# First MLP of a fused attention and two-MLP kernel: softmax steps, squares and conversions in other slots, and all four sums of a half batch cleared by ACT

## The chip, the cores and the metric

The kernel runs on one core of a Trainium2 chip. The metric is device time in microseconds of one execution; lower is better. The engines are TensorE (PE, with its weight loads as PEld), VectorE (DVE), ScalarE (ACT) and SyncE (SP), which issues the DMAs. Each takes its instructions in the order in which the program has them.

## The reference

Attention in two steps (32 packed queries per head gather k and v, then q attends to the result), an MLP with squared ReLU, and an MLP with x times sigmoid(1.702 x). Everything is float32; w_in, w_out and their second pair come in as 64-bit numbers.

```
s = scale * q k^T;  a = exp(s - max);  a = a / (sum(a) + 1e-9)       # sm_attn
p_packed = sm_attn(p, k, v)            # 8 batches, 8 heads, 32 x 64
out = sm_attn(q, p_packed, p_packed)   # 8 batches, 8 heads, 576 x 64
x = out as (4608, 512)
h = max(x @ w_in, 0);  x = (h * h) @ w_out          # w_in 512 x 2048, w_out 2048 x 512
h = x @ w_in2;  out = (h * sigmoid(1.702 h)) @ w_out2
```

## The kernel before

A matrix product in float32 is made from three products of split numbers (`prod`, L79): hi by hi, hi by lo and lo by hi. The split of a number is an ACT copy (hi) and a DVE subtraction (lo), as in `split` (L74).

**First MLP, up to 788 us.** The product of p_packed with w_in is folded first: for each batch `m_step` (L364) makes M, four pieces f of 512 columns, from p_packed and w_in, so that h is M times the attention weights a. Tokens go by half batches of 288, the 2048 hidden columns by 16 blocks `fc` of 128. A *slot* is one (half batch, block). The main loop at the end of the function issues, slot by slot: the split of the block two slots ahead (`gsplit`, L391), the first product, ReLU and square of the block three slots ahead (`mm1`, L378: six matmuls into a bank, relu L386, square L388, both on ACT), the second product of this slot's block (`mm2`, L395: twelve matmuls, three into each of four banks `y`), and then what the plan holds for the slot. After the last block of a half batch `mm2` empties the four banks into `ysb` and stores it. The next block's first matmul into a bank waits for that.

From batch 2 on a batch is 32 slots: slots 0 to 15 for the first half, 16 to 31 for the second. Beside them runs the attention of the next batch, in the slots that a list `steps` (L742) gives, counted from the batch's first slot: `s1`, `s1b` (first scores and their exponentials), `tr`, `pv`, `t2` (p_packed and its transposes), then for each half `s2a` (scores of q, transposed and less their maximum, on DVE), `s2b` (exponential on ACT, L344, then sum, reciprocal, multiplication and transpose on DVE, L346 to L355) and `s2c` (split into a), and `m_step` for the four f. In batches 0 and 1 (table `first`, L684) the halves are cut into eight blocks and w_in and w_out are still being converted from 64 bits; there `ysb` is a sum with what was stored before (L414, DVE).

The w_in pieces for `m_step` are read back by `load_win` into three buffers, two pieces per f: n = 0 to 2 ahead, the others in the slots of the `m_step`s that free a buffer.

Also beside the batches run the conversions of the second MLP's weights (`convert`): two ACT and four DVE instructions each (L118 to L129), and the sums and splits of weight parts (`unit_sums`, `unit_hi` on ACT, L190, `unit_lo` on DVE, L195, each followed by a store to w_d from one of three buffers). They stand in slots that are not 14, 15 or 0 of 16.

**Second MLP, from 788 us.** Tokens go by five pairs of blocks (512 or 384 each side) with a seven-product scheme: `y_sum` makes four differences of the input on DVE (T1 to T4, L481), `y_hi` and `y_lo` split them (L489 on ACT, L492 on DVE), `mm_a` and `mm_b` are the products, `keep_a` (L554) empties a bank on ACT, and `g_sum`, `g_hi`, `g_lo` (L511, L516, L492) make the operands of the second product. `at2(t0 + dt, ...)` puts a step dt product-steps from the pair's first.

Of the kernel before, what the change touches and what calls it, by code (L numbers as in the profile page):

```python
# [13 lines left out]
AF = mybir.ActivationFunctionType  # L14
ALU = mybir.AluOpType
# [8 lines left out]
HS = S // 2  # L24
NFC = DFF // P
# [18 lines left out]
def fused_kernel(ctx, tc, qT, kT, vv, pT, w_in, w_out, w_in2, w_out2, out):  # L44
# [7 lines left out]
    nc = tc.nc  # L52
# [337 lines left out]

    def gsplit(b, hf, fc, seg):  # L391
# [3 lines left out]
    def mm2(b, hf, fc, seg):  # L395
# [281 lines left out]
    wps = []  # L677


    for f, *a in (*loads(0)[:6], (ahead,), loads(0)[6], (ahead,), (load_q, 0, 0, 0), (load_q, 0, 1, 0), (ahead,),  # L680
                  (load_q, 0, 2, 0), (load_q, 0, 3, 0), (ahead,), *((load_q, 0, hp, 1) for hp in range(4))):
        at(S0, f, *a)

    first = {  # L684
# [15 lines left out]
        5: [(tr, 1, 0), (convert,)],  # L700
# [14 lines left out]
        22: [(convert,)],  # L715
        23: [(convert,)],
        25: [(convert,)],
        26: [(convert,)],
        27: [(convert,), (convert,)],
        30: [(m_step, 0, 3), (convert,)],  # L720
        33: [(convert,)],
        35: [(convert,)],
        43: [(m_step, 1, 2)],
        46: [(m_step, 1, 3)],
    }
    for s, steps in first.items():
        for f, *a in steps:
# [67 lines left out]
    for p in range(NP2):  # L797
# [93 lines left out]
```

## Time and profile before

| | us |
|---|---|
| median of 3 runs | 1491.49 (1489.2 to 1492.52) |
| the profiled execution, by its own time | 1491.68 |
| its span, first to last instruction | 1489.5 |
| busy: PE, DVE, ACT | 1435.9, 973.9, 846.6 |
| mean granted TensorE clock, share of full | 0.984 |

The span is what the trace covers; some 2 us of the device time lie around it. Busy times of different engines lie beside each other and are not to be added. PE's busy time counts matmuls whose ends are modelled, so waits show better than busy shares do. All times below are from the start of the span.

### The profile page before, as it was taken

The page shows a single profiled execution, that of the slowest core. Times are in us where ns is not written, and L with a number is a line of the kernel's source. Part 1 is how long each engine was busy: PE and PEld are TensorE (multiplying, and loading weights), DVE is VectorE, ACT ScalarE, POOL GpSimd, SP SyncE. Part 2 cuts the span into 40 slices and gives each one's busy share as a digit, 9 for nine tenths or more (in the row PEclk, how much of TensorE's full clock was granted, in tenths as well). Part 3 has the DMA queues.
Part 4 walks back from the last instruction along what each step waited for, and adds up shares of the span by engine and source line. Part 5 has one row for each costly group of instructions (what it writes and reads, how often), then busy time and mean ns, then how long its engine had stood idle before and what let it go on. Part 6 is the DMA issues. An engine that isn't in the chain of part 4 may idle for free.

```text
span 1489.5 us, 25122 instructions
## 1 busy us (share of the span) xinstructions
PE 1435.9 (96%) x9786; PEld 1281.5 (86%) x9786; DVE 973.9 (65%) x1684; ACT 846.6 (57%) x1760; POOL 0.7 (0%) x6
## 2 busy tenths in 40 slices
PE   7899999999999998999999999999999999999998
PEld 4678989888898897889998888788878888999998
DVE  6898465756756666573235687668775776677585
ACT  4888667567676766665565463446344634454452
POOL 0000000000000000000000000000000000000000
PEclk8999999999999999999999999999999999999999
DMA  9756657476465664633044566556765576677775
GB/s 310 248 171 219 206 180 235 149 234 199 163 215 185 213 205 161 204 134 123 17 151 164 197 218 250 207 188 221 263 215 197 211 244 237 248 286 284 256 285 174
DMA packets 110774, 307.95 MB, mean 207 GB/s; under 512 B 9024, under 2 KB 52032, under 8 KB 96576
## 3 DMA queue, kind: packets, MB, share of 16 engines
q1 hardware_dynamic: 110656, 306.35, 60.3%
q8 instruction: 77, 1.26, 0.3%
q14 instruction: 41, 0.34, 0.1%
HBM read 250.94 MB, written 55.38 MB: 206 GB/s over the span
## 4 chain that ended last, share of the span: by engine, by line
PE 74%; DVE 14%; ACT 5%; DMA 4%; issue 2%; SPq 0%; ACTq 0%; DVEq 0%
PE h L85 33%; PE y L85 22%; PE o L85 14%; DVE hid L511 2%; PE m L256 2%; ACT g L516 2%; DMA w_d<-wc 1%; DVE g L492 1%; PE s L256 1%; DVE yT L481 1%; DVE y L492 1%; DMA wA<-w_d 1%; DVE o L593 1%; DVE gh L77 1%; PE pv L314 1%
## 5 line engine op out<-in xcount | busy, mean ns | idle before, releaser
L85 PE MATMUL y<-gh,wo 128*128 128x288 f32 x3072 | 461.2, 300 | 24.3 <-ACT ysb L418 14.7
L85 PEld LDWEIGHTS y<-gh,wo 128*128 128x128 f32 x3072 | 431.1, 192 | 28.6 <-ACT ysb L418 17.1
L85 PE MATMUL h<-y,wA 128*128 128x512 f32 (+1 forms) x1680 | 350.2, 368 | 4.7 <-ACT r L554 3.4
L85 PE MATMUL o<-g,wB 128*128 128x512 f32 (+1 forms) x1680 | 348.9, 367 | 0.3 <-DMA wB<-w_d 0.3
L85 PEld LDWEIGHTS h<-y,wA 128*128 128x128 f32 x1680 | 305.4, 188 | 46.6 <-ACT r L554 5.5
L85 PEld LDWEIGHTS o<-g,wB 128*128 128x128 f32 x1680 | 305.7, 188 | 39.8 <-DMA wB<-w_d 0.6
L85 PE MATMUL h<-a,M 128*128 128x288 f32 x1536 | 263.2, 307 | 10.7 <-ACT a L360 3.8
L85 PEld LDWEIGHTS h<-a,M 128*128 128x128 f32 x1536 | 221.8, 193 | 56.4 <-issue 27.6
L516 ACT ACTIVATE g<-hid 128x1024 fp32r<-128x1024 f32 (+1 forms) x140 | 132.8, 971 | 146.8 <-DVE hid L511 120.3
L77 DVE TENSOR_TENSOR gh<-gf,gh 128x288 fp32r<-128x288 f32 x256 | 114.9, 452 | 112.6 <-ACT gh L76 112.3
L492 DVE TENSOR_TENSOR g<-hid,g 128x1024 fp32r<-128x1024 f32 (+1 forms) x140 | 152.7, 1115 | 54.5 <-ACT g L516 53.6
L386 ACT ACTIVATE r<-h 128x288 f32<-128x288 f32 x256 | 103.8, 406 | 102.8 <-PE h L85 102.3
L554 ACT ACTIVATE r<-h 128x512 f32<-128x512 f32 (+1 forms) x120 | 66.5, 554 | 116.6 <-PE h L85 114.5
L562 DVE TENSOR_TENSOR hid<-h,r 128x512 f32<-128x512 f32 (+1 forms) x120 | 76.0, 634 | 74.4 <-PE h L85 62.6
L388 ACT ACTIVATE gf<-r 128x288 f32<-128x288 f32 x256 | 113.9, 445 | 8.1
L76 ACT ACTIVATE gh<-gf 128x288 fp32r<-128x288 f32 x256 | 111.8, 437 | 1.8
L572 DVE TENSOR_TENSOR hid<-hid,sg 128x512 f32<-128x512 f32 (+1 forms) x120 | 75.9, 632 | 47.2 <-ACT sg L568 47.2
L373 DVE TENSOR_TENSOR M<-m,M 128x512 fp32r<-128x512 f32 x64 | 43.6, 690 | 72.5 <-ACT M L371 71.6
L568 ACT ACTIVATE sg<-hid 128x512 f32<-128x512 f32 (+1 forms) x120 | 70.2, 585 | 31.1 <-DVE hid L562 30.9
L511 DVE TENSOR_TENSOR hid<-hid 128x1024 f32<-128x1024 f32 (+1 forms) x60 | 66.3, 1112 | 0.0
L371 ACT ACTIVATE M<-m 128x512 fp32r<-128x512 f32 x64 | 37.2, 594 | 41.6 <-PE m L256 41.6
L190 ACT ACTIVATE wc<-sum 128x256 fp32r<-128x256 f32 x64 | 26.1, 408 | 31.4 <-DMA w_d<-wc 31.2
(94 smaller groups left out, 939.6 us busy)
## 6 DMA issues: line engine op xcount, KB each, us to landing
wB<-w_d SPq DMA_DIRECT2D x70, 1024.0 KB, 4.9
wA<-w_d SPq DMA_DIRECT2D x40, 1024.0 KB, 4.8
wA<-w_d SPq DMA_DIRECT2D x40, 768.0 KB, 6.2
win<-win_d SPq DMA_DIRECT2D x56, 512.0 KB, 5.0
w_d<-wc SPq DMA_DIRECT2D x112, 256.0 KB, 3.8
k<-in_kT SPq DMA_DIRECT2D x32, 288.0 KB, 4.8
y_d<-ysb SPq DMA_DIRECT2D x16, 576.0 KB, 3.7
v<-in_vv SPq DMA_DIRECT2D x16, 512.0 KB, 7.3
```

Source lines behind the costliest of these rows:

```text
L76: nc.scalar.activation(hi, src, AF.Copy)
L77: nc.vector.tensor_tensor(out=lo, in0=src, in1=hi.bitcast(F32), op=ALU.subtract)
L85: nc.tensor.matmul(ps, w, x, start=start and i == 0, stop=stop and i == n - 1, skip_group_check=more)
L386: nc.scalar.activation(r, ps[:, :HS], AF.Relu)
L388: nc.scalar.activation(g, r, AF.Square)
L492: nc.vector.tensor_tensor(out=t[:, :, 1, :n], in0=src, in1=t[:, :, 0, :n].bitcast(F32), op=ALU.subtract)
L511: nc.vector.tensor_tensor(out=t, in0=i0, in1=i1, op=ALU.subtract)
L516: nc.scalar.activation(t[:, :, 0, :PAIRS[p]], gop[p, i, g, "src"], AF.Copy)
L554: nc.scalar.activation(t[:, 0, :n], bank[p, c, "1"][:, :n], AF.Copy)
L562: nc.vector.tensor_tensor(out=hid(p, c, blk), in0=bank[p, c, b][:, :n], in1=part[p, c, r][:, 0, :n], op=ALU.add)
L568: nc.scalar.activation(t, bank[p, c, "1"][:, :n] if blk == 2 else hid(p, c, blk), AF.Sigmoid, scale=GELU)
L572: nc.vector.tensor_tensor(out=hid(p, c, blk), in0=bank[p, c, "1"][:, :n] if blk == 2 else hid(p, c, blk), in1=part.pop((p, c, "sg", blk)), ...
```

## The change

Clearing of the banks: from batch 2 on, all four banks of a half batch leave through ACT copies; before, banks 1 and 3 left through DVE copies. Squares: for blocks 2, 3 and 13 the square moves from ACT to DVE, from batch 2 on. Softmax steps: other slots in `steps`. Conversions: some stand a slot earlier or later, or before another step of their slot, in the first 35 slots. Loads at the start: the second half of the first q comes before the second v. Second MLP: T1, T3 and the first split stand earlier, T2 and one more split by a step. `CALM` names the slots that were already used (1 to 13 of 16), so it moves nothing.

```
+SQ_DVE = (2, 3, 13)
+CALM = (1, 2, 3, 4, 5, 6, 7, 8, 9, 10, 11, 12, 13)
...
-        nc.scalar.activation(g, r, AF.Square)
+        if fc in SQ_DVE and b > 1:
+            nc.vector.tensor_tensor(out=g, in0=r, in1=r, op=ALU.mult)
+        else:
+            nc.scalar.activation(g, r, AF.Square)
...
-                elif d % 2 and b > 1:
-                    nc.vector.tensor_copy(y[:, d, :], accs[d][:, :HS])
...
-        -6: [(convert,), (s2a, 0, 0)],
-        -5: [(s2b, 0, 0), (convert,), (warm, 14)],
+        -6: [(convert,), (s2a, 0, 0), (convert,)],
+        -5: [(s2b, 0, 0), (warm, 14)],
...
-            steps = [(0, s1, 0), (2, s1, 1), (3, s1b), (5, tr, 0), (6, pv, 0), (7, tr, 1), (8, pv, 1), (9, t2),
-                     (10, s2a, 0), (11, s2b, 0), (13, s2c, 0), (13, s2a, 1), (14, s2b, 1), (17, s2c, 1)]
-
-            steps += [(s, m_step, f) for f, s in enumerate((18, 21, 25, 29))]
+            steps = [(0, s1, 0), (1, s1, 1), (4, s1b), (7, tr, 0), (8, pv, 0), (8, tr, 1), (9, pv, 1),
+                     (10, t2), (12, s2a, 0), (16, s2b, 0), (17, s2c, 0), (17, s2a, 1), (20, s2b, 1), (26, s2c, 1)]
+
+            steps += [(s, m_step, f) for f, s in enumerate((19, 21, 26, 29))]
...
-        for dt, f, x in ((-14, y_hi, 1), (-14, y_sum, "T1"), (-13, y_lo, 1), (-13, y_sum, "T2"), (-12, y_sum, "T3"),
...
+        for dt, f, x in ((-17, y_sum, "T1"), (-16, y_hi, 1), (-16, y_sum, "T3"), (-12, y_sum, "T2"),
+                         (-12, y_lo, 1), (-10, y_hi, 2), (-9, y_lo, 2), (-8, y_hi, 6), (-8, y_lo, 6),
```

The lines of the changed kernel have numbers up to eight higher. In the pieces below a name such as gh_3_1_2 is batch 3, half 1, block 2; s2t4_1 is the softmax tile of batch 4, half 1; ysb_3_0 the sums of batch 3, half 0, and y_3_0_2 bank 2 of them; wc and x_p, with raw_p, belong to conversions.

ACT before, slots 14 to 16 of batch 3:

```order
L76 ACTIVATE gh_3_1_0_5097<-gf_3_1_0_5060 128x288
L386 ACTIVATE r_3_1_1_5107<-h_3_1_1_5100 128x288
L388 ACTIVATE gf_3_1_1_5109<-r_3_1_1_5107 128x288
L344 ACTIVATE s2t4_1_5086<-s2t4_1_5086 128x576
L76 ACTIVATE gh_3_1_1_5132<-gf_3_1_1_5109 128x288
L386 ACTIVATE r_3_1_2_5142<-h_3_1_2_5135 128x288
L388 ACTIVATE gf_3_1_2_5144<-r_3_1_2_5142 128x288
L418 ACTIVATE ysb_3_0_5158<-y_3_0_0_0_4489 128x288
L418 ACTIVATE ysb_3_0_5158<-y_3_0_2_0_4497 128x288
L76 ACTIVATE gh_3_1_2_5164<-gf_3_1_2_5144 128x288
```

and with the change, slots 14 to 17:

```order
L78 ACTIVATE gh_3_1_0_5071<-gf_3_1_0_5053 128x288
L388 ACTIVATE r_3_1_1_5081<-h_3_1_1_5074 128x288
L393 ACTIVATE gf_3_1_1_5083<-r_3_1_1_5081 128x288
L78 ACTIVATE gh_3_1_1_5099<-gf_3_1_1_5083 128x288
L388 ACTIVATE r_3_1_2_5109<-h_3_1_2_5102 128x288
L421 ACTIVATE ysb_3_0_5125<-y_3_0_0_0_4489 128x288
L421 ACTIVATE ysb_3_0_5125<-y_3_0_1_0_4493 128x288
L421 ACTIVATE ysb_3_0_5125<-y_3_0_2_0_4497 128x288
L421 ACTIVATE ysb_3_0_5125<-y_3_0_3_0_4501 128x288
L78 ACTIVATE gh_3_1_2_5131<-gf_3_1_2_5111 128x288
L388 ACTIVATE r_3_1_3_5141<-h_3_1_3_5134 128x288
L346 ACTIVATE s2t4_0_5021<-s2t4_0_5021 128x576
```

The exponential of the softmax (L344, now L346) stood in front of the copies of two banks; it stands behind the copies of all four, and the square between relu and copies has gone.

DVE before, in the same slots, from the subtraction that this exponential reads:

```order
L339 TENSOR_TENSOR s2t4_1_5086<-s2t4_1_5086,s2st4_1_5087 128x576
L77 TENSOR_TENSOR gh_3_1_0_5097<-gf_3_1_0_5060,gh_3_1_0_5097 128x288
L195 TENSOR_TENSOR wc5_5_5091<-sum5_4961,wc5_5_5091 128x2x128
L346 TENSOR_REDUCE s2st4_1_5087<-s2t4_1_5086 128x18
L348 TENSOR_SCALAR s2st4_1_5087<-s2st4_1_5087 128x18
L350 RECIPROCAL s2st4_1_5087<-s2st4_1_5087 128x18
L352 TENSOR_TENSOR s2t4_1_5086<-s2t4_1_5086,s2st4_1_5087 128x576
L355 STREAM_TRANSPOSE s2x4_1_5130<-s2t4_1_5086 128x576
L77 TENSOR_TENSOR gh_3_1_1_5132<-gf_3_1_1_5109,gh_3_1_1_5132 128x288
L416 COPY ysb_3_0_5158<-y_3_0_1_0_4493 128x288
L416 COPY ysb_3_0_5158<-y_3_0_3_0_4501 128x288
L77 TENSOR_TENSOR gh_3_1_2_5164<-gf_3_1_2_5144,gh_3_1_2_5164 128x288
```

and with the change:

```order
L79 TENSOR_TENSOR gh_3_1_0_5071<-gf_3_1_0_5053,gh_3_1_0_5071 128x288
L197 TENSOR_TENSOR wc5_5_5069<-sum5_4948,wc5_5_5069 128x2x128
L79 TENSOR_TENSOR gh_3_1_1_5099<-gf_3_1_1_5083,gh_3_1_1_5099 128x288
L391 TENSOR_TENSOR gf_3_1_2_5111<-r_3_1_2_5109 128x288
L79 TENSOR_TENSOR gh_3_1_2_5131<-gf_3_1_2_5111,gh_3_1_2_5131 128x288
L391 TENSOR_TENSOR gf_3_1_3_5143<-r_3_1_3_5141 128x288
L348 TENSOR_REDUCE s2st4_0_5022<-s2t4_0_5021 128x18
L350 TENSOR_SCALAR s2st4_0_5022<-s2st4_0_5022 128x18
L352 RECIPROCAL s2st4_0_5022<-s2st4_0_5022 128x18
L354 TENSOR_TENSOR s2t4_0_5021<-s2t4_0_5021,s2st4_0_5022 128x576
L357 STREAM_TRANSPOSE s2x4_0_5166<-s2t4_0_5021 128x576
L79 TENSOR_TENSOR gh_3_1_3_5168<-gf_3_1_3_5143,gh_3_1_3_5168 128x288
```

The copies of two banks stood behind the five instructions that end the softmax; there are none any more, two squares (L391) stand in their place, and the end of the softmax (now L348 to L357, of the first half, s2t4_0) comes after them.

DVE in the second MLP, before the second pair's first product; yT1 and yT2 are differences T1 and T2, yst1_0 on the left of the arrow is T3, g0_4_1 the lo part of an operand of the first pair, hid0_2 the subtraction in front of it. Before:

```order
L511 TENSOR_TENSOR hid0_2_10659<-hid0_2_10659 128x2x512
L492 TENSOR_TENSOR g0_4_2_11326<-hid0_2_10659,g0_4_2_11326 128x2x512
L481 TENSOR_TENSOR yT1_1_11341<-yst1_0_11225 128x1024
L492 TENSOR_TENSOR y1_1_11339<-yst1_0_11225,y1_1_11339 128x2x512
L481 TENSOR_TENSOR yT2_1_11352<-yst1_1_11236,yT1_1_11341 128x1024
L511 TENSOR_TENSOR hid0_3_10802<-hid0_3_10802 128x2x512
L481 TENSOR_TENSOR yst1_0_11225<-yst1_1_11236,yst1_0_11225 128x2x512
L492 TENSOR_TENSOR g0_4_3_11368<-hid0_3_10802,g0_4_3_11368 128x2x512
L492 TENSOR_TENSOR y1_2_11377<-yst1_1_11236,y1_2_11377 128x2x512
```

and with the change:

```order
L514 TENSOR_TENSOR hid0_1_10516<-hid0_1_10516 128x2x512
L484 TENSOR_TENSOR yT1_1_11309<-yst1_0_11225 128x1024
L495 TENSOR_TENSOR g0_4_1_11307<-hid0_1_10516,g0_4_1_11307 128x2x512
L514 TENSOR_TENSOR hid0_2_10659<-hid0_2_10659 128x2x512
L484 TENSOR_TENSOR yst1_0_11225<-yst1_1_11236,yst1_0_11225 128x2x512
L495 TENSOR_TENSOR g0_4_2_11331<-hid0_2_10659,g0_4_2_11331 128x2x512
L514 TENSOR_TENSOR hid0_3_10802<-hid0_3_10802 128x2x512
L484 TENSOR_TENSOR yT2_1_11359<-yst1_1_11236,yT1_1_11309 128x1024
L495 TENSOR_TENSOR y1_1_11319<-yst1_0_11225,y1_1_11319 128x2x512
L495 TENSOR_TENSOR g0_4_3_11368<-hid0_3_10802,g0_4_3_11368 128x2x512
L495 TENSOR_TENSOR y1_2_11377<-yst1_1_11236,y1_2_11377 128x2x512
```

T1 and T3 stood behind the last operands but one; each now stands between a subtraction and the lo part that waits for ACT to split it.

## Rows read from the trace of the kernel before

**Rows 1.** Page, part 1: busy time, share of the span, instructions.

```profile
PE 1435.9 (96%) x9786; PEld 1281.5 (86%) x9786; DVE 973.9 (65%) x1684; ACT 846.6 (57%) x1760; POOL 0.7 (0%) x6
```

**Rows 2.** Waits of PE, 150 to 788 us: total, times, longest.

```profile
PE y L85 <- ACT ysb L418: 10.6, 7, 2.2
PE y L85 <- DVE ysb L416: 7.5, 5, 1.6
...
PE y L85 <- DVE yp L414: 2.1, 1, 2.1
```

**Rows 3.** Windows, slots 15 to 17: batch 1, 2, sum 2-6, 7.

```profile
193.62:203.15 9.53, 7.45 (x56) 7.22 (x55) 6.99 (x16) 5.54 (x13) 0.00 (x0) 1.00 0.60 185
283.79:297.38 13.59, 10.22 (x57) 9.76 (x56) 9.19 (x20) 6.87 (x17) 0.00 (x0) 0.75 0.24 83
...
sum 64.91, PE 48.73 PEld 46.26 DVE 43.04 ACT 31.99 POOL 0.00; mean PE 9.75 PEld 9.25 DVE 8.61 ACT 6.40 POOL 0.00
...
750.65:757.78 7.13, 7.13 (x56) 7.13 (x55) 2.21 (x5) 4.50 (x11) 0.00 (x0) 1.00 0.50 148
```

**Rows 4.** Timeline, slots 15 and 16 of batch 3: start, length, instruction.

```profile
383.25 0.68 ACT L344 ACTIVATE s2t<-s2t 128x576 f32<-128x576 f32 x1 [3.71 <-DVE s2t L339]
...
383.96 0.75 DVE L346 TENSOR_REDUCE s2st<-s2t 128x18 f32<-128x576 f32 x1
...
384.94 0.69 ACT L418 ACTIVATE ysb<-y 128x288 f32<-128x288 f32 x2
...
385.39 0.43 PEld L85 LDWEIGHTS y<-gh,wo 128*128 128x128 f32 x3 [2.28 <-ACT ysb L418]
...
386.06 0.78 DVE L355 STREAM_TRANSPOSE s2x<-s2t 128x576 f32<-128x576 f32 x1
...
387.09 0.81 DVE L416 COPY ysb<-y 128x288 f32<-128x288 f32 x2
...
387.60 2.08 PE L85 MATMUL y<-gh,wo 128*128 128x288 f32 x9 [1.55 <-DVE ysb L416]
```

**Rows 5.** Windows, slots 30 to 32: batch 1, 2, sum 2 and 5.

```profile
236.61:244.59 7.98, 7.98 (x72) 7.35 (x71) 5.03 (x12) 4.76 (x12) 0.00 (x0) 1.00 1.08 354
330.84:341.61 10.77, 8.51 (x72) 7.42 (x71) 4.80 (x12) 5.85 (x16) 0.00 (x0) 1.00 0.90 310
...
sum 20.70, PE 17.02 PEld 14.83 DVE 9.13 ACT 10.91 POOL 0.00; mean PE 8.51 PEld 7.42 DVE 4.57 ACT 5.46 POOL 0.00
```

**Rows 6.** Waits of the whole span: ACT for stores.

```profile
ACT wc L190 <- DMA w_d<-wc: 31.2, 16, 4.4
```

**Rows 7.** Waits of PE from 788 us on (second MLP).

```profile
PE h L85 <- ACT r L554: 3.4, 3, 1.2
```

**Rows 8.** Timeline of the second MLP, end of the first pair.

```profile
927.32 1.23 DVE L492 TENSOR_TENSOR g<-hid,g 128x1024 fp32r<-128x1024 f32 x1 [1.19 <-ACT g L516]
...
941.56 1.06 ACT L489 ACTIVATE y<-yT 128x1024 fp32r<-128x1024 f32 x1 [3.50 <-DVE yT L481]
...
943.16 3.01 PE L85 MATMUL h<-y,wA 128*128 128x512 f32 x12 [1.09 <-ACT r L554]
```

**Rows 9.** Timeline of PE, batch 3: products with w_in.

```profile
395.31 1.09 PE L256 MATMUL m<-win,ppT 64*32 64x512 f32 x16
...
403.67 1.09 PE L256 MATMUL m<-win,ppT 64*32 64x512 f32 x16
```

**Rows 10.** DMA issues at 300.2 and 583.8 us: KB, us to landing.

```profile
win<-win_d SPq DMA_DIRECT2D x1, 512.0 KB, 6.5
...
win<-win_d SPq DMA_DIRECT2D x1, 512.0 KB, 3.6
```

**Rows 11.** Groups by line, DVE, 240 to 620 us: busy, mean ns.

```profile
L77 DVE TENSOR_TENSOR gh<-gf,gh 128x288 fp32r<-128x288 f32 x128 | 57.4, 451 | 42.6 <-ACT gh L76 42.6
L373 DVE TENSOR_TENSOR M<-m,M 128x512 fp32r<-128x512 f32 x32 | 22.1, 691 | 37.1 <-ACT M L371 36.4
```

**Rows 12.** Timeline of the start: first exponential, second softmax.

```profile
22.11 0.69 ACT L344 ACTIVATE s2t<-s2t 128x576 f32<-128x576 f32 x1 [2.64 <-DVE s2t L339]
```

More of the change, by code (lines that the diff above doesn't have):

```diff
@@ L677, in fused_kernel @@
     wps = []
-    for f, *a in (*loads(0)[:6], (ahead,), loads(0)[6], (ahead,), (load_q, 0, 0, 0), (load_q, 0, 1, 0), (ahead,),
-                  (load_q, 0, 2, 0), (load_q, 0, 3, 0), (ahead,), *((load_q, 0, hp, 1) for hp in range(4))):
+    for f, *a in ((load_p, 0), (load_k, 0, 0), (load_k, 0, 1), (load_k, 0, 2), (load_k, 0, 3), (load_v, 0, 0),
+                  (ahead,), (load_q, 0, 0, 1), (load_v, 0, 1), (ahead,), (load_q, 0, 0, 0), (load_q, 0, 1, 0),
+                  (ahead,), (load_q, 0, 2, 0), (load_q, 0, 3, 0), (ahead,), (load_q, 0, 1, 1), (load_q, 0, 2, 1),
+                  (load_q, 0, 3, 1)):
         at(S0, f, *a)
@@ L694, in fused_kernel @@
         -1: [(s2c, 0, 1), (convert,)],
-        0: [(s1, 1, 0), (convert,)],
+        0: [(convert,), (s1, 1, 0)],
         1: [(s1, 1, 1), (convert,)],
@@ L699, in fused_kernel @@
         4: [(m_step, 0, 1), (convert,)],
-        5: [(tr, 1, 0), (convert,)],
+        5: [(convert,), (tr, 1, 0)],
         6: [(pv, 1, 0), (convert,), (tr, 1, 1)],
@@ L704, in fused_kernel @@
         9: [(s2b, 1, 0)],
-        10: [(s2c, 1, 0), (convert,)],
-        11: [(convert,), (m_step, 1, 0)],
+        10: [(convert,), (s2c, 1, 0)],
+        11: [(m_step, 1, 0), (convert,)],
         13: [(convert,)],
-        14: [(convert,)],
+        14: [(s2a, 1, 1), (convert,)],
         15: [(m_step, 1, 1)],
-        16: [(convert,), (s2a, 1, 1)],
+        16: [(convert,)],
         17: [(convert,)],
@@ L714, in fused_kernel @@
         21: [(m_step, 0, 2)],
-        22: [(convert,)],
         23: [(convert,)],
+        24: [(convert,)],
         25: [(convert,)],
         26: [(convert,)],
-        27: [(convert,), (convert,)],
-        30: [(m_step, 0, 3), (convert,)],
+        27: [(convert,)],
+        29: [(convert,)],
+        30: [(convert,), (m_step, 0, 3)],
         33: [(convert,)],
@@ L723, in fused_kernel @@
         43: [(m_step, 1, 2)],
-        46: [(m_step, 1, 3)],
+        47: [(m_step, 1, 3)],
     }
@@ L757, in fused_kernel @@
             at(s0 + max(at_w if n < 3 else ws[(n - 3) // 2], 40 if b == 1 and f > 1 else 0), load_win, b, f, n % 2)
-    calm = [s for s in range(45, SB - 2 * NFC) if s % 16 not in (14, 15, 0)]
+    calm = [s for s in range(45, SB - 2 * NFC) if s % 16 in CALM]
     for u in range(2 * KC + 1):
         s = calm[8 * u:8 * u + 8]
+        assert len(s) == 8
         convert(s[0])
@@ L815, in fused_kernel @@
             at2(t0 - 26 + h, y_load, p, h)
-        for dt, f, x in ((-14, y_hi, 1), (-14, y_sum, "T1"), (-13, y_lo, 1), (-13, y_sum, "T2"), (-12, y_sum, "T3"),
-                         (-10, y_hi, 2), (-9, y_lo, 2), (-8, y_hi, 6), (-7, y_lo, 6), (-6, y_hi, 5), (-6, y_sum, "T4"),
-                         (-5, y_lo, 5), (-4, y_hi, 7), (-3, y_lo, 7), (-2, y_hi, 4), (-1, y_lo, 4), (1, y_hi, 3), (2, y_lo, 3)):
+        for dt, f, x in ((-17, y_sum, "T1"), (-16, y_hi, 1), (-16, y_sum, "T3"), (-12, y_sum, "T2"),
+                         (-12, y_lo, 1), (-10, y_hi, 2), (-9, y_lo, 2), (-8, y_hi, 6), (-8, y_lo, 6),
+                         (-7, y_hi, 5), (-6, y_sum, "T4"), (-6, y_lo, 5), (-4, y_hi, 7), (-3, y_lo, 7),
+                         (-2, y_hi, 4), (-1, y_lo, 4), (1, y_hi, 3), (2, y_lo, 3)):
             at2(t0 + dt, f, p, x)
```

## The prediction

> **What bounds the kernel now.** I read the page first, then the waits of TensorE (PE), then the same three slots of every batch side by side, then the instructions inside them. A slot is one block of w_out for one half batch; 32 slots make a batch, and slot 15 is the last block of its first half.
>
> TensorE is busy for 96% of the span [rows 1], so what counts is the little in which it waits or is slow. In the stretch of the first MLP with five batches in it, nearly all of its waiting is for the four sums of a half batch to leave their banks: 10.6 us for ACT copies, 7.5 us for DVE copies, 2.1 us for DVE additions [rows 2]. Where it happens is seen when slots 15 to 17 are cut out of each batch: 7.13 us in the last batch, which has no attention beside it, but 64.91 us for the five batches 2 to 6 together, where five times 7.13 would be 35.65 [rows 3]. So 29.3 us, 2% of the run, lie in three slots of five batches. The waits are not all of it: the granted clock falls there (0.75 in the first of them, against 1.00 in the last batch), that is, the engine stood still and was then run at 1.2 instead of 2.4 GHz for a while. Of the 29.3 at most 18.1 (10.6 + 7.5) are waits, so at least 11 are the slow clock.
>
> The instructions tell why [rows 4]. ACT's next one in line is the exponential of the softmax (L344), and it has waited 3.71 us for DVE's subtraction (L339); the copies of banks 0 and 2 (L418) stand behind it and start at 384.94, and TensorE goes on 2.05 us late. It does three products, then waits 1.55 us for bank 1, since DVE's copies (L416) stand behind the rest of the softmax (L346 to L355, 383.96 to 386.84).
>
> **The change part by part.** Times are set against the profiled execution: span 1489.5, run 1491.7, which is 0.2 over the median of the three runs shown.
>
> Banks and softmax. In 24 places (six batches, two halves, two banks) a DVE copy becomes an ACT copy, the exponential of the first half moves from slot 11 to 16 and of the second from 14 to 20, and three of every 16 squares go from ACT to DVE. I follow slot 15 with rows' durations. 54 products in 7.13 us are 0.132 each: twelve take 1.59, the six between them 0.79. Take 0 as the start of slot 15's twelve. ACT does the relu of the block before (0.4, about as long as a copy), then a copy every 0.35 (0.69 for two [rows 4]); bank d is complete at 0.4 (d + 1). So the copies end near 0.8, 1.2, 1.6 and 2.0. TensorE wants bank 0 again at 2.38 and bank 3 at 3.57. ACT could be 1.5 us late and nothing would wait, and nothing in front of the copies waits for the softmax any more: the exponential stands behind them, on an input that DVE subtracted four slots earlier. I take all 29.3 us back, clock included, since with no wait nothing is left that made it fall.
>
> A rule to set against this is in the Trainium skill, TensorE: Matmul & The Clock Gate, "A second HAM failure mode: psum-queue depth-cycling": frequent very short idles between matmul groups are enough to keep the clock swinging. By it the slow clock could stay though the long waits go, and the part would give 18 and not 29; it is the third rival. The stretch from 330.84 has 2.3 us without a product and the clock at 1.00 [rows 5], which speaks against it.
>
> Batch 1 has the same fault with additions in place of copies (L414, still on DVE): 9.53 against 7.13 [rows 3]. The softmax step in front of them (L346 to L355) now comes one slot after them. I take 2.4 us.
>
> Slots 30 to 32. Two changes of batch take 20.70 us where two others' length, 7.98 each, would make 15.96 [rows 5]. There ACT waits for a buffer of converted weights whose store has not landed (31.2 us in all, up to 4.4, mostly hidden [rows 6]). Positions of those conversions do not change, so this stays. A square less stands before the copies, 0.4 us each time: 0.9 back. Bounds: nothing, or the whole excess of 4.7.
>
> Second MLP. Between pairs TensorE waits for ACT to clear a bank, 3.4 us in three places [rows 7]: 1.09 at 943.16, with ACT held 3.50 us by the last of DVE's four differences (L481) [rows 8]. Two of the three earlier ones now stand where DVE waited 1.2 us for ACT between its subtractions (927.32), so the last comes about 2.4 us sooner, more than the 1.09. I take 3.3 of 3.4; bounds 0 and 3.4.
>
> Now what it adds. (a) The first product with w_in of a batch moves from slot 18 to 19, the second stays in 21. The second needs a piece whose load can start only when the first is done. Now 7.27 us lie between them (396.40 to 403.67 [rows 9]); a slot less leaves 4.9, and 0.5 more until the half that reads this piece: 5.4. The six loads of the batches took 6.5 us (the first shown), 3.6 (the last) and between these [rows 10], all but the first short of 5.4. So 1.1 us in one batch: 1.0; bounds 0 and 6.6 (1.1 in all six). (b) Faster slots leave less time per transfer, and the last w_in piece goes out a slot later, just in front of the next batch's k: a longer wait for the stores of [rows 6]. No row shows it; nothing at one end, a second 31.2 on top at the other, of which 4.7 reach TensorE now: 0 to 5, I take 1.5. (c) Two steps share slot 8 (pv and the next transpose). The transpose needs a bank that DVE clears at once if it is idle, as it is there; if not, one of its instructions is in front, 0.78 at most in [rows 4]. 0 to 4.7 in six batches, I take 0. (d) DVE gets 36 squares, which the trace does not have on DVE; L77, of the same shape and with two inputs, takes 0.45 [rows 11]. It loses 24 copies of 0.41 [rows 4]; ACT the reverse. Neither is on the path outside the places above. (e) At the start DVE has three conversion steps ahead of the subtraction that the first exponential waits for (2.64 us now [rows 12]), and they no longer fill the time after it. Total work is the same; I lose 0.7, between 1 back and 2 lost. The other moved conversions of the first 40 slots I take at nothing: same count, on an ACT and a DVE that run one behind the other there.
>
> Sum: -29.3 - 2.4 - 0.9 - 3.3 + 1.0 + 1.5 + 0.7 = -32.7, and 1491.7 - 32.7 = 1459.
>
> **The rivals.**
> 1. The reload of w_in decides slot 21. For: a slot less, and a busier memory after the stall is gone. Against: the loads but one had a microsecond or more to spare. With all six at 6.5 us it is 6.6 instead of 1.0: 1465; with the clock falling behind half of them, 3 us each, 1474. I put it at 1469. The Trainium skill, DMA: Bandwidth & Descriptors, "Latency and other measured facts", gives memory latency as rising from 0.2 to 2 us under high load, which would lengthen these loads; no run here separates that.
> 2. The stores decide slots 27 to 32, so that ACT's waits grow in more batches: 5 us of (b) and 0.9 not gained, with a slow-clock tail: 1466 to 1472, say 1469.
> 3. The waits go but the clock still falls: 18.1 instead of 29.3, thus 1470.
> 4. Slower: DVE becomes the bound in slots 16 to 21. Into six slots of some 17.5 us (six of 2.38 and three more steps like the 1.09 of [rows 9]) now fall both softmax ends (2.9 each, 383.96 to 386.84 [rows 4]), four parts of M (0.69 each) and seven gh and squares (0.45 each [rows 11]), 11.7 us, and a dozen more of 0.4 to 0.8, about 7: 18.7. A gh is wanted two slots after it is put in line, so 4.8 us of delay are free. If DVE is later than that, TensorE waits in each batch as it does now: 5.85 us (29.3 / 5) in six batches is 35, more than all gains, so 1494. Against: the list starts with DVE idle and my sum ends 1.2 us late, not 4.8.
> 5. Nothing happens: the copies wait for something else. Speaks against it that [rows 4] name the two releasers.
>
> **How the numbers follow.** Forecast 0.66 with 1453 to 1465 of its own; rival 1 0.11, rival 2 0.12, rival 3 0.05, rival 4 0.04, rival 5 0.02. A measurement of this kernel can tell about 0.2%, 3 us. Faster: 0.66 + 0.11 + 0.12 + 0.05 = 0.94; same 0.02; slower 0.04. The range takes the forecast's own and most of rivals 1 to 3: 1453 to 1474.
>
> **What would show it.** Right: slots 15 to 17 near 7.1 us in every batch at clock 1.00, no TensorE wait for ysb, none for L414 in batch 1, no wait for ACT's bank copy between pairs. Wrong: a TensorE wait for a w_in load at slot 21 (rival 1), longer ACT waits for w_d (rival 2), clock under 1.00 without waits (rival 3), TensorE waiting for gh in slots 16 to 24 with DVE solid (rival 4), or a first product of the first MLP more than 2 us later than now.

## The result and the profile after

| | before | changed | ratio, 95% interval |
|---|---|---|---|
| first timing, median of 4 runs each | 1490.65 us | 1453.20 (1451.16 to 1453.56) | 0.9745 [0.9728, 0.9762] |
| the changed kernel timed again (4 runs, 7 of before) | 1491.98 us | 1450.82 (1449.47 to 1453.83) | 0.9727 [0.9709, 0.9746] |

Faster, as forecast, and by more: 32.7 us were predicted, the first ratio makes 38.0 of 1490.65 us, which is 1452.6, just below the low end of the range (1453), and the second makes 40.7. The terms of the sum, set against two profiles of the changed kernel (executions of 1451.2 and 1451.3 us, against 1491.7 before), show which were too small. A stage is cut by the first product with w_out of its slots; its change is against the one profile of before. Slot 0 of batch 2 and batch 7 from its slot 1 on, which stand in no line, did not change.

| stage | predicted | first profile | second profile |
|---|---|---|---|
| start and slots 0 to 31 | +0.7 | -0.1 | -0.7 |
| batch 1 | -2.4 | -2.6 | -2.6 |
| slots 1 to 17 of batches 2 to 6 | -29.3 | -28.8 | -29.4 |
| slots 18 to 26 (reload of w_in) | +1.0 | +1.7 | +2.0 |
| slots 27 to 32 (stores) | -0.9 + 1.5 | -4.5 | -3.8 |
| second MLP | -3.3 | -6.0 | -5.6 |
| sum (spans: 1489.55 to 1449.37 and 1449.52) | -32.7 | -40.2 | -40.0 |

The page of the changed kernel answers [rows 1]: 14.1 us less of TensorE's busy time with the same 9786 matmuls, since fewer of them ran at half the clock: by the trace's clock 27.3 us between batch 2 and the second MLP before, none now.

```profile
PE 1421.8 (98%) x9786; PEld 1271.6 (88%) x9786; DVE 980.5 (68%) x1696; ACT 842.1 (58%) x1748; POOL 0.7 (0%) x6
```

The waits of TensorE between 148 and 753 us, the first MLP from batch 1 on (total, times, longest), answer [rows 2]:

```profile
PE tr_b L305 <- DVE ppb L320: 0.3, 1, 0.3
PE y L87 <- ACT ysb L421: 0.2, 1, 0.2
PE m L258 <- DMA win<-win_d: 0.2, 1, 0.2
```

Of 20.2 us of waits for the banks 0.2 are left. Slots 15 to 17 of batch 1, 2, 5 and 7 (window, length, busy time and instructions of PE, PEld, DVE, ACT, POOL, granted clock, DMA share, GB/s) and then the sum of batches 2 to 6 answer [rows 3]:

```profile
191.35:200.55 9.20, 9.20 (x88) 7.57 (x87) 6.67 (x14) 5.39 (x13) 0.00 (x0) 1.00 0.58 187
280.35:288.33 7.98, 7.98 (x72) 7.35 (x71) 5.18 (x12) 6.05 (x14) 0.00 (x0) 1.00 0.37 127
546.47:554.85 8.38, 8.27 (x73) 7.41 (x72) 7.58 (x18) 5.81 (x16) 0.00 (x0) 1.00 0.49 164
716.45:723.58 7.13, 7.13 (x56) 7.13 (x55) 2.29 (x5) 4.49 (x11) 0.00 (x0) 1.00 0.51 155
```

```profile
sum 40.30, PE 40.19 PEld 36.81 DVE 28.95 ACT 29.55 POOL 0.00; mean PE 8.04 PEld 7.36 DVE 5.79 ACT 5.91 POOL 0.00
```

The clock is 1.00 in all, and the five batches take 40.30 us instead of 64.91. They take 7.98 and not the 7.13 of batch 7 since the scores of the second half (`s2a`, 16 small products) now stand in slot 17 and no longer in slot 13; slots 1 to 14 are as much shorter, so the table takes 1 to 17 together. Batch 5 has 0.40 more, with DVE at 7.58 of 8.38. Inside batch 3 the timeline (start, length, engine, instruction, idle before) answers [rows 4]:

```profile
370.75 1.21 ACT L421 ACTIVATE ysb<-y 128x288 f32<-128x288 f32 x3
...
371.35 0.95 PE L87 MATMUL h<-a,M 128*128 128x288 f32 x6
...
372.14 1.75 PE L87 MATMUL y<-gh,wo 128*128 128x288 f32 x12
...
372.65 0.68 ACT L346 ACTIVATE s2t<-s2t 128x576 f32<-128x576 f32 x1
...
373.36 0.75 DVE L348 TENSOR_REDUCE s2st<-s2t 128x18 f32<-128x576 f32 x1
...
375.45 0.78 DVE L357 STREAM_TRANSPOSE s2x<-s2t 128x576 f32<-128x576 f32 x1
```

ACT's copies (L421, three of the four in this row) follow each other from 370.75 on with nothing in front of them that waits, TensorE runs on without an idle, and the exponential (L346) comes after them with no idle either: its input is long there. The end of the softmax on DVE (373.36 to 376.2) has only a later operand behind it.

The slots 30 to 32 of batches 2 and 5 together, and ACT's waits for stores over the span, answer [rows 5, 6]:

```profile
sum 16.44, PE 16.21 PEld 14.72 DVE 8.69 ACT 9.55 POOL 0.00; mean PE 8.11 PEld 7.36 DVE 4.35 ACT 4.78 POOL 0.00
```

```profile
ACT wc L192 <- DMA w_d<-wc: 20.8, 13, 4.8
```

16.44 instead of 20.70, and 20.8 instead of 31.2 us of waits: the stores got better, where I had them get worse. The reload of w_in shows in batch 4, at the second product of `m_step` (answering [rows 9]):

```profile
475.51 1.06 PE L258 MATMUL m<-win,ppT 64*32 64x512 f32 x8
476.74 1.06 PE L258 MATMUL m<-win,ppT 64*32 64x512 f32 x8 [0.17 <-DMA win<-win_d]
```

It is cut in two halves, and the second starts 1.23 us after the first, where it is 0.45 in batches 3, 5 and 6. The idle that the row names is 0.17, yet slots 18 to 26 of this batch are 1.2 longer. Matmul ends are modelled, and here a wait inside a group was worth more than its idle time: the second half started 0.8 us late and 1.2 were lost. In the second MLP the waits of [rows 7] are gone; the one left is for a load:

```profile
PE h L87 <- DMA wA<-w_d: 0.7, 1, 0.7
```

and the end of the first pair, where [rows 8] had a wait of 1.09:

```profile
903.75 1.22 DVE L484 TENSOR_TENSOR yT<-yst,yT 128x1024 f32<-128x1024 f32 x1
...
905.09 1.06 ACT L492 ACTIVATE y<-yT 128x1024 fp32r<-128x1024 f32 x1 [4.35 <-DVE yT L484]
...
906.34 1.52 PE L87 MATMUL o<-g,wB 128*128 128x512 f32 x6
...
907.70 2.65 PE L87 MATMUL h<-y,wA 128*128 128x512 f32 x11
```

The last difference (L484) now ends 2.7 us ahead of the group of twelve that needs a bank free (907.70). ACT still waits for it, 4.35 us, but is done with its split in time to clear the bank, and TensorE goes from the product at 906.34 into the group without an idle.

### The profile page after: what moved, and what is told of

It is laid out like the page before. It is cut to its first block, busy times and chain, and to the rows that moved or that the text cites. A ratio compares the mean times of both kernels' runs of the same rounds, so it can differ in the third digit from the quotient of the medians.

```text
span 1449.4 us, 25048 instructions
## 1 busy us (share of the span) xinstructions
PE 1421.8 (98%) x9786; PEld 1271.6 (88%) x9786; DVE 980.5 (68%) x1696; ACT 842.1 (58%) x1748; POOL 0.7 (0%) x6
## 4 chain that ended last, share of the span: by engine, by line
PE 91%; DVE 4%; DMA 3%; ACT 2%; issue 1%; SPq 0%; DVEq 0%; ACTq 0%
PE h L87 37%; PE y L87 26%; PE o L87 24%; PE m L258 2%; PE s L258 1%; DMA w_d<-wc 1%; PE pv L316 1%; DMA k<-in_kT 1%; DMA wA<-w_d 1%; PE tr_a L304 0%; DMA win<-win_d 0%; DVE wo L153 0%; DVE gh L79 0%; DVE x_wo L131 0%; DVE x_wo L129 0%
## 5 line engine op out<-in xcount | busy, mean ns | idle before, releaser
L87 PE MATMUL y<-gh,wo 128*128 128x288 f32 x3072 | 451.2, 296 | 3.5 <-ACT ysb L421 2.3
L87 PEld LDWEIGHTS y<-gh,wo 128*128 128x128 f32 x3072 | 423.7, 189 | 4.6 <-ACT ysb L421 3.0
L87 PE MATMUL h<-a,M 128*128 128x288 f32 x1536 | 258.9, 303 | 8.8 <-ACT a L362 3.2
L87 PEld LDWEIGHTS h<-a,M 128*128 128x128 f32 x1536 | 218.6, 191 | 53.2 <-issue 27.0
L393 ACT ACTIVATE gf<-r 128x288 f32<-128x288 f32 x220 | 97.9, 445 | 7.0
L258 PE MATMUL m<-win,ppT 64*32 64x512 f32 x512 | 39.6, 615 | 4.3 <-DVE s2t L337 4.1
```

What stands on the lines that cost most here:

```text
L87: nc.tensor.matmul(ps, w, x, start=start and i == 0, stop=stop and i == n - 1, skip_group_check=more)
L258: nc.tensor.matmul(ps[r][32 * hp:32 * hp + 32, :n], w(hp)[rows], xx, start=True, stop=True)
```

## The experiments

Each was timed beside runs of the kernel before on its own chip, so ratios are compared. The changed kernel itself gave 0.9745 and 0.9727, so ratios that differ by 0.002 can't be told apart, and most of what follows is read from the lengths of stages, which are from one profile each.

**1. The softmax slots alone (kernel before).**

```
-steps = [(0, s1, 0), (2, s1, 1), (3, s1b), ... (10, s2a, 0), (11, s2b, 0), (13, s2c, 0), (13, s2a, 1), (14, s2b, 1), (17, s2c, 1)]
+steps = [(0, s1, 0), (1, s1, 1), (4, s1b), ... (12, s2a, 0), (16, s2b, 0), (17, s2c, 0), (17, s2a, 1), (20, s2b, 1), (26, s2c, 1)]
```

> The kernel before with only the first attention steps and the softmax steps of batches 2 on in their new slots; banks 1 and 3 still leave through DVE, all squares on ACT, m_step in its old slots. Theory 1 (what stands in front of the copies decides): nearly all of the 28.9 us of slots 15 to 17 comes back although DVE still copies two banks, so 1459 to 1463 us, and TensorE has no wait for ysb over 0.5 us. Rival (the engine of the copies decides: DVE is the slow one to get to them): DVE's 7.5 us of waits and a part of the slow clock stay, 1470 us or more.

1461.5 us, ratio 0.9788 [0.977, 0.9806]. Windows on slots 15 to 17 of batches 2 and 5 and the sum of 2 to 6, then the waits of TensorE from 150 to 757 us:

```profile
280.68:288.66 7.98, 7.98 (x73) 7.35 (x72) 5.07 (x12) 5.53 (x13) 0.00 (x0) 1.00 0.36 125
...
549.29:557.87 8.58, 8.38 (x72) 7.42 (x71) 7.66 (x18) 6.46 (x16) 0.00 (x0) 1.00 0.46 160
...
sum 40.50, PE 40.30 PEld 36.82 DVE 28.58 ACT 28.50 POOL 0.00; mean PE 8.06 PEld 7.36 DVE 5.72 ACT 5.70 POOL 0.00
```

```profile
PE h L85 <- ACT r L386: 1.7, 1, 1.7
PE y L85 <- ACT ysb L418: 1.6, 2, 0.9
...
PE y L85 <- DVE ysb L416: 0.2, 1, 0.2
```

40.50 against the changed kernel's 40.30: the whole of the stall goes, with DVE still copying two banks and every square on ACT. One wait of 0.9 for ACT's copies is longer than expected, but the two stand at changes of batch, not in slot 16; the longer comes after the wait for the relu of 1.7 (slots 30 to 32 of batch 2 are still 11.16 us long). So theory 1 holds. What is missing to the changed kernel, 10.1 us by the profiles, lies elsewhere: 5.7 in the second MLP and 4.2 in slots 27 to 32.

**2. The banks alone (kernel before).**

```
-                elif d % 2 and b > 1:
-                    nc.vector.tensor_copy(y[:, d, :], accs[d][:, :HS])
```

> The kernel before with only the banks changed: from batch 2 on all four leave through ACT; softmax, squares and m_step as before. Theory 1 (what stands in front of the copies decides): the exponential still holds ACT, so the first wait of about 2 us in each of five batches stays, DVE's second wait of 1.5 us goes, and the clock still falls: 1478 to 1488 us, slots 15 to 17 over 9 us in each of the batches 2 to 6. Rival (the engine decides): about 1462 us and no waits over 0.5 us.

1474.32 us, ratio 0.9876 [0.9854, 0.9897]: between the two. Windows of slots 15 to 17 of batches 2 to 6, and the waits for the banks:

```profile
283.56:294.31 10.75, 8.93 (x57) 8.70 (x56) 8.26 (x18) 7.19 (x18) 0.00 (x0) 0.84 0.31 105
377.76:387.20 9.44, 7.39 (x56) 7.16 (x55) 7.63 (x16) 6.56 (x17) 0.00 (x0) 1.00 0.49 171
467.84:476.02 8.18, 7.39 (x56) 7.16 (x55) 6.40 (x14) 6.57 (x17) 0.00 (x0) 1.00 0.31 111
557.50:568.71 11.21, 8.95 (x56) 8.72 (x55) 8.45 (x18) 7.92 (x21) 0.00 (x0) 0.85 0.33 119
650.81:660.03 9.22, 7.40 (x56) 7.17 (x55) 7.40 (x16) 6.56 (x17) 0.00 (x0) 1.00 0.34 124
sum 48.80, PE 40.07 PEld 38.91 DVE 38.14 ACT 34.80 POOL 0.00; mean PE 8.01 PEld 7.78 DVE 7.63 ACT 6.96 POOL 0.00
```

```profile
PE y L85 <- ACT ysb L416: 10.6, 7, 2.3
```

ACT's waits are all there (10.6 us, as in [rows 2]), DVE's 7.5 are gone, as theory 1 said. What it had wrong is the clock: with one wait instead of two in a row it fell in batches 2 and 5 only (0.84 and 0.85) and stayed at 1.00 in three. So DVE's second wait cost its 7.5 us and most of the slow clock too: TensorE's busy time in these slots is 40.07 us and not the 48.73 of [rows 3]. What sets the two batches apart isn't shown: 1.82 us of wait in both batch 2 and batch 6, and the clock fell in one.

**3. The old slots of m_step (changed kernel).**

```
-            steps += [(s, m_step, f) for f, s in enumerate((19, 21, 26, 29))]
+            steps += [(s, m_step, f) for f, s in enumerate((18, 21, 25, 29))]
```

> The changed kernel with m_step back in its old slots 18, 21, 25 and 29. Both theories: the first product with w_in in slot 18 gives the reload a slot more, so the 2 us that slots 18 to 26 of batches 2 and 4 and slots 15 to 17 of batch 5 are over their undisturbed length go. Theory A (the slots of m_step, which put loads of w_in between the stores on SP's queue, decide how late the stores land): 4.5 us come back as ACT's waits in slots 30 to 32 of batches 2 and 5, net 2 to 3 us slower than the changed kernel, 1455 to 1457. Theory B (the stores were late since the stall of slots 15 to 17 held up the conversions and what follows them): slots 30 to 32 stay at 8.0 to 8.5 us, and the time is 1451 to 1452.

1456.73 us, ratio 0.9753 [0.9734, 0.9773]. Slots 30 to 32 of batches 2 and 5 are 11.93 and 9.17 us (8.46 and 7.98 in the changed kernel, 10.77 and 9.94 before), and batches 2 to 6 together 446.6 instead of 442.0. Batch 4 gets its 1.2 us back (25.12 in slots 18 to 26), but batch 2 takes 26.73: there the reload is later still, with 7.0 us from issue to landing. Theory A as to the stores; as to the reload only in batch 4.

**4. The old order of differences in the second MLP (changed kernel).**

```
-        for dt, f, x in ((-17, y_sum, "T1"), (-16, y_hi, 1), (-16, y_sum, "T3"), (-12, y_sum, "T2"), (-12, y_lo, 1), ...
+        for dt, f, x in ((-14, y_hi, 1), (-14, y_sum, "T1"), (-13, y_lo, 1), (-13, y_sum, "T2"), (-12, y_sum, "T3"), ...
```

> The changed kernel with the differences and splits of the second MLP in their old order. Theory A (the whole gain of the second MLP, 5.9 us by the two traces, is this order's, each wait being worth 0.3 us more than its idle time shows): 5.2 to 5.9 us slower than the changed kernel, about 1459, with waits at the starts of three pairs and two of 0.3 to 0.4 near the last. Theory B (only the three waits for ACT's bank copy belong to it, 3.4 us; the rest is from what runs before, as buffers and loads that arrive earlier): about 1456.6, and the two short waits near the last pair stay away.

1455.67 us, ratio 0.9748 [0.9732, 0.9765]. The second MLP's waits of TensorE, and the end of its first pair:

```profile
PE h L87 <- ACT r L557: 3.4, 3, 1.2
PE h L87 <- DVE o L596: 0.4, 1, 0.4
```

```profile
906.58 1.23 DVE L484 TENSOR_TENSOR yT<-yst,yT 128x1024 f32<-128x1024 f32 x1
...
906.90 1.52 PE L87 MATMUL o<-g,wB 128*128 128x512 f32 x6
...
907.92 1.06 ACT L492 ACTIVATE y<-yT 128x1024 fp32r<-128x1024 f32 x1 [3.50 <-DVE yT L484]
...
909.52 3.06 PE L87 MATMUL h<-y,wA 128*128 128x512 f32 x12 [1.10 <-ACT r L557]
```

By the profiles the second MLP is 4.3 us longer than the changed kernel's (from the first product to the span's end: 699.9 against 695.6). The three waits for ACT's bank copy lose 1.43, 1.39 and 1.45 us for idles of 1.10, 1.09 and 1.22, the one for DVE 0.63 for 0.40; that is 4.9, and the changed kernel has in its place a wait of 0.7 for a load that is absent here. So A was right that the short wait near the last pair belongs to the order and that a wait is worth 0.2 to 0.3 more than its idle, but not as to the whole. The ten profiles with the new order have 694.6 to 696.3 us here, this run 699.9, and the three profiles of the kernel before and of runs 1 and 2, which have the old order in it, 701.4 to 701.6. The rest of the 6.0 is therefore not this order's; in part it is waits for loads (0.8 at 1261.86 and 0.3 at 1431.08 before), and what else is open.

**5. The squares on ACT (changed kernel).**

```
-        if fc in SQ_DVE and b > 1:
+        if False and fc in SQ_DVE and b > 1:
```

> The changed kernel with every square on ACT again. Theory 1 (only what stands in front of the copies decides, and with the exponential gone one square more, 0.45 us, does not make them late): 1452 to 1455 us, slots 15 to 17 at 7.98 us in each of the batches 2 to 6 as in the changed kernel. Rival (ACT needs the room for four copies): copies late by 0.4 us or more in each half batch, more of ACT's waits for stores reach TensorE, 1457 us or more.

1451.01 us, ratio 0.973 [0.9714, 0.9747]. Slots 15 to 17 are 7.98 in all five batches. The squares on DVE give nothing that can be measured, not in slots 30 to 32 either: 17.3 us in batches 2 and 5 together, 16.4 and 17.1 in the changed kernel's two profiles.

**6. The old start (changed kernel).** The load order and the whole table `first` of before, of which two lines:

```
-        -6: [(convert,), (s2a, 0, 0), (convert,)],
-        -5: [(s2b, 0, 0), (warm, 14)],
+        -6: [(convert,), (s2a, 0, 0)],
+        -5: [(s2b, 0, 0), (convert,), (warm, 14)],
```

> The changed kernel with the loads, conversions and early steps of the start (slots -10 to 47) in their old order. Theory A (the start as a whole neither gains nor loses, since ACT and DVE run one behind the other there and have the same work): the first product of slot 64 at 238.5 to 240 us, as in the traces with the new order (238.7, 239.9, 239.3), and 1452 to 1455 us. Rival (the new order costs 1.3 us before slot 0 and gives 1.4 in slots 0 to 31 and 2.5 in batch 1): slot 64 at 241 us or later, 1455 to 1457.

1453.17 us, ratio 0.9744 [0.973, 0.9759]; slot 64 at 239.4 us. Theory A. The start is worth nothing that can be measured, and its length differs between runs of one code: slot 64 starts at 238.0 to 240.3 in nine profiles with the new order.

**7. The reload a slot later (changed kernel).**

```
-            steps += [(s, m_step, f) for f, s in enumerate((19, 21, 26, 29))]
+            steps += [(s, m_step, f) for f, s in enumerate((19, 22, 26, 29))]
```

> The changed kernel with the second product with w_in of a batch in slot 22 instead of 21. Theory A (the reload of w_in is what slots 18 to 26 of batches 2 and 4 and slots 15 to 17 of batch 5 wait for): 1.8 to 2.1 us come back, 1451 to 1452. Rival (loads that go out a slot later meet the stores behind them, as with the old slots): slots 30 to 32 of batches 2 and 5 grow by 1 to 4 us and eat it, 1453 to 1457.

1451.48 us, ratio 0.9731 [0.9713, 0.9749]. Slots 18 to 26 are at 25.07 us in all batches: 1.9 back, the reload was the cause. But slots 30 to 32 of batch 2 grew,

```profile
322.79:333.03 10.24, 8.55 (x73) 7.43 (x71) 4.52 (x11) 5.28 (x16) 0.00 (x0) 1.00 0.84 279
```

and batch 4 lost 0.7 in slots 27 to 29 to an operand of DVE's. The sum of batches 2 to 6 is 442.1 against 442.0: rival and theory in equal parts.

**8. Both (6 and 7).**

> The changed kernel with both: the old order at the start and the second product with w_in in slot 22. If both are worth what the theories A of the two single runs say, 1450 to 1452 us, the fastest of all; by the rivals 1455 us or more.

1454.17 us, ratio 0.9751 [0.9735, 0.9767]. Not the fastest: slot 64 starts at 243.5 us, with 6.8 us more at half the clock between 60 us and slot 64 than in run 6, by the trace's clock, and the rest is as in run 7. No combination tried here beats the changed kernel by more than runs of it differ.

**9 and 10. One of the old m_step slots at a time (changed kernel).**

```
-            steps += [(s, m_step, f) for f, s in enumerate((19, 21, 26, 29))]
+            steps += [(s, m_step, f) for f, s in enumerate((18, 21, 26, 29))]     # run 9
+            steps += [(s, m_step, f) for f, s in enumerate((19, 21, 25, 29))]     # run 10
```

> The changed kernel with only the first product with w_in of a batch back in slot 18. On SP's queue its two loads of w_in then stand in front of a store that stood before them. Theory (this puts the store 1 MB of loads later, and ACT, which waits for the store's buffer, late until slot 30): slots 30 to 32 of batch 2 at 10.8 to 12 us and of batch 5 at 9.0 to 10 as with all four old slots, about 4 us more than the changed kernel, less 1 to 2 us that the reload no longer costs: 1454 to 1457. Rival (the third product, slot 25 or 26, and its load decide): batch 2 at 8.0 to 9.5, batch 5 at 8.0, 1450 to 1453.

> The changed kernel with only the third product with w_in of a batch back in slot 25. Theory (slot 18 of the first product made the stores late, not this one): slots 30 to 32 of batch 2 at 8.0 to 9.5 us and of batch 5 at 8.0, 1450 to 1454. Rival (the third product decides): 10.8 us or more in batch 2, 9 or more in batch 5, 1455 to 1458.

1452.37 us, ratio 0.9735 [0.972, 0.975], and 1455.7, ratio 0.9757 [0.9742, 0.9771]. Beside them on the same chip the changed kernel took 1449.47 to 1453.83 (run 12): run 9 (1450.97 to 1453.81) can't be told from it by its time, run 10 (1454.73 to 1456.45) can. SP's queue around slot 19 of batch 2, in the changed kernel and in run 9:

```profile
292.32 0.54 SPq L144 DMA_DIRECT2D raw_p<-in_w_in  x1
293.06 0.44 SPq L200 DMA_DIRECT2D w_d<-wc  x1
293.60 0.97 SPq L241 DMA_DIRECT2D win<-win_d  x2
294.67 2.18 SPq L200 DMA_DIRECT2D w_d<-wc  x2
```

```profile
291.75 0.54 SPq L144 DMA_DIRECT2D raw_p<-in_w_in  x1
292.38 1.02 SPq L241 DMA_DIRECT2D win<-win_d  x2
293.51 1.94 SPq L200 DMA_DIRECT2D w_d<-wc  x3
```

In the changed kernel a store (w_d) goes out ahead of the two loads of w_in, in run 9 it goes behind them. The conversion on ACT that waits for a store's buffer, in the same two:

```profile
297.81 0.42 ACT L192 ACTIVATE wc<-sum 128x256 fp32r<-128x256 f32 x1 [1.13 <-DMA w_d<-wc]
```

```profile
301.31 0.42 ACT L192 ACTIVATE wc<-sum 128x256 fp32r<-128x256 f32 x1 [5.90 <-DMA w_d<-wc]
```

1.13 us and 5.90. In both, ACT goes on as the store lands, which takes 4.7 us from its issue in the changed kernel and 7.7 behind the loads; the rest of the difference is that the store goes out 0.5 later and that ACT is there 1.3 sooner. ACT is then late with the conversions, and so are SP's next loads and stores, up to the change of batch, where the last conversion waits 3.2 us for a store instead of 2.1. The windows of slots 30 to 32 of batch 2 in runs 9 and 10:

```profile
322.69:334.23 11.54, 10.02 (x72) 8.46 (x71) 4.42 (x10) 5.17 (x15) 0.00 (x0) 0.85 0.78 255
```

```profile
324.23:334.73 10.50, 8.58 (x72) 7.46 (x71) 4.71 (x11) 5.47 (x16) 0.00 (x0) 1.00 0.89 303
```

11.54 us, with the clock falling (0.85), and 10.50; 8.46 in the changed kernel. So the mechanism of run 9 is shown, but the theory that it alone decides fell: the third product a slot earlier does nearly as much, and in run 3 both together hardly more than one. In run 10, in slot 25, a store that went out ahead of the load of w_in goes out behind it again, and the next load of raw weights goes out 9.9 us after the start of slot 24 instead of 5.4 (9.9 also before and in run 3, 7.2 in run 9); the last conversion then waits 3.3 us. That it is the same mechanism is likely, but no run takes it apart. Over the span ACT's waits for stores go with the first product: 31.1 to 34.4 us in the five profiles that have it in slot 18 (before and runs 1, 2, 3, 9), 17.5 to 25.8 in the nine others, run 10 (25.2) among them. Batch 5 (7.98 and 8.75) tells nothing, since the same changed kernel has 7.98 and 8.65 in its two profiles. In all, batches 2 to 6 were 3.1 and 3.8 us longer than in the changed kernel's first profile.

**11. The exponential in front again, with an input that is ready (changed kernel).**

```
-                     (10, t2), (12, s2a, 0), (16, s2b, 0), ...
+                     (10, t2), (12, s2a, 0), (14, s2b, 0), ...
```

> The changed kernel with the exponential of the first half in slot 14 instead of 16, so that it stands again in front of the copies on ACT, and the rest of that softmax in front of two operands on DVE. Its subtraction stays in slot 12. Theory 1 (the copies were late since what stood in front of them had to wait for DVE's subtraction, one slot old; an exponential whose input is ready costs ACT only its 0.68 us): slots 15 to 17 within 0.5 us of 7.98 in each of batches 2 to 6, no wait for ysb over 0.5 us, 1450 to 1455. Rival (its place in front is enough): waits for ysb of 0.7 us or more in each of the five batches, with a lower clock in some, 1457 us or more.

1453.06 us, ratio 0.9741 [0.9727, 0.9756]. Windows of slots 15 to 17 of batches 2 and 5, and the wait of TensorE for an operand in batch 5:

```profile
281.52:289.50 7.98, 7.98 (x73) 7.35 (x71) 4.77 (x13) 6.18 (x15) 0.00 (x0) 1.00 0.37 127
...
547.85:556.72 8.87, 8.41 (x73) 7.42 (x72) 7.61 (x17) 5.06 (x14) 0.00 (x0) 1.00 0.48 155
```

```profile
PE y L87 <- DVE gh L79: 0.5, 1, 0.5
```

7.98 in four batches and 8.87 in batch 5, where 8.5 at most was expected, and no wait for ysb. The exponential may stand in front of ACT's copies; what held them was its wait of up to 3.7 us for a subtraction put in line one slot before it [rows 4]. No bank leaves through DVE in this run, so what the rest of that softmax does in front of DVE's copies was not tested.

**12. The changed kernel again.**

> The changed kernel once more, unaltered, for a second profile: it is to tell which terms repeat. Expected 1451 to 1454 us. Slots 15 to 17 (7.98 us) and batch 5's slots 30 to 32 should repeat to 0.1 us. The start (first product of slot 0 and slots 0 to 14), slots 30 to 32 of batch 2 (8.0 to 9.4 so far) and the waits for loads in the second MLP (0 or 0.7 to 1.1 so far) should differ by about 1 us each.

1450.82 us. Slots 15 to 17 repeat to 0.2 us in the sum (40.11); slots 30 to 32 of batch 2 repeat (8.47), those of batch 5 do not (8.65), against what was expected. The second MLP's one wait is again for a load:

```profile
PE h L87 <- DMA wA<-w_d: 0.8, 1, 0.8
```

## Why the prediction was right, and where it was wrong

**The banks (right).** 29.3 predicted, 28.8 and 29.4 measured, clock included; the clock was at 1.00 in all five batches. Slots 15 to 17 alone took 7.98 us (8.38 in batch 5) and not the 7.1 that was to show it, since the working left out that `s2a` moves into slot 17. Its split was off too: two of the seven waits for ACT's copies, 1.0 us each, stand at changes of batch (338.28 and 621.06), so 16.2 of the 29.3 were waits and 13 the slow clock. Runs 1 and 2 sharpen the reason: to move the softmax steps is enough, and for ACT's copies what counts is the distance between subtraction and exponential (run 11). Banks on ACT and squares on DVE, which the working followed instruction by instruction, are not needed for it, though the banks alone give back 16.1 of the 24.6 us of these slots (run 2). Rival 3, that the clock would fall without the waits, is out; run 2 shows the clock staying up in three of five batches even with a wait of 0.8 to 2.1 us in each. By the rule of the Trainium skill weighed there (TensorE: Matmul & The Clock Gate, "A second HAM failure mode: psum-queue depth-cycling") very short idles could have kept the clock swinging here. No row read here shows many such idles, so the rule itself was not tested.

**Batch 1 and the start (right).** -2.6 against -2.4, and it is the softmax steps': the batch takes 90.3 us in run 1 and 92.7 in run 2, against 92.8 before and 90.2 with the change. The start came out between -0.1 and -0.7 against +0.7, and run 6 shows that it can't be told from no change.

**The reload (right mechanism, too small).** +1.7 and +2.0 against +1.0: two batches instead of one. The loads took 5.4 and 5.5 us there (batches 2 and 4), and the room for them was 5.2 and 4.7 instead of 5.4: in batch 4 SP issues a load of raw weights just ahead. A stop inside the group also cost 0.4 to 0.5 more than the load was late. Run 7, which gives the room back, takes 1.9 of it away. Term (c), put at nothing, was one wait of 0.3 in slot 8 of batch 3.

**The stores (wrong).** The step that failed is "Positions of those conversions do not change, so this stays", with (b) on top of it: +0.6 predicted, -3.8 to -4.5 measured, which is 4.4 to 5.1 of the 7.3 to 7.5 us by which the sum fell short of the profiles. The conversions did keep their slots; the order on SP's queue did not keep. The first and third product with w_in move from slots 18 and 25 to 19 and 26, which the list of the change names only in its lines of code. They take their loads with them, and on SP's queue a load is ahead of or behind a store of the same slot (runs 3, 9 and 10). I had counted the moved loads for their own landing and, the last piece, for standing just in front of the next batch's k, not for the stores that they were moved past on the queue. With the old slots the whole gain of slots 27 to 32 goes (run 3: 86.1 us, 85.9 before, 81.4 with the change). Rival 2, the same thing with the other sign, is out. The 0.9 for the squares can't be seen (run 5).

**The second MLP (right mechanism, too small).** -3.3 against -5.6 to -6.0. I took the idle of three waits as their price. Run 4 shows that each is worth 0.2 to 0.3 more (4.3 for the three) and that a fourth, 0.4 at the last pair, had the same cause (0.6). The rest, about 1 us, is in part loads that landed at other times, and in part open.

**DVE as the bound (rival 4, out).** The changed kernel's list of waits from 148 us on has none for an operand of DVE's in slots 16 to 21 of any batch. The 0.4 in batch 5's slots 15 to 17 (a weight load waits 0.34 for gh there, at 549.24), the 0.5 of run 11 and 0.2 of run 9 in the same batch, and the 0.4 in slot 29 of batch 4 of run 7 are the signs that DVE is near.

## What to carry to other kernels

When a cheap instruction waits on an in-order engine, look first at how far its input's producer stands ahead of it in the program: one slot was too little here, two were enough, and its place in front of others then cost nothing in four batches of five. When a step is moved, list what its DMAs are moved past on the issuing queue, also by a single place; that decided 3 to 4 us here. Price a TensorE wait by the length of the stage with it and without it, not by the idle that the row shows.

## What the runs showed of the hardware that was not expected

- Two waits of 0.8 to 2.2 and 1.2 to 1.6 us in one slot brought the clock down in five batches of five; the first of them alone (0.8 to 2.3 us) did so in two of five, and equal waits (1.82 us) came out either way. At the change of batch 2, two waits of 1.0 to 1.7 and 0.5 to 1.0 us, a slot apart, did so in two of seven runs (3 and 9).
- An idle of TensorE of 1.1 us in the records was worth 1.4 us of time, one of 0.17 inside a group of sixteen products 1.2.
- One store moved behind 1 MB of loads took 7.7 us to land instead of 4.7, and a wait of 1.1 us on ACT became one of 5.9.
